# First attention of a fused attention and mixture-of-experts kernel: the sums' addition, the turn of 1/sum, and the place of the mixture's normalization

## The chip, the cores and the metric

The kernel runs on one core of one Trainium2 chip. The metric is the device time of one execution in microseconds: the median of three runs. The core has TensorE (matrix products into PSUM), VectorE, ScalarE and GpSimd (elementwise work), and queues that move data between HBM and SBUF; each engine works through its own instructions in order and waits on semaphores for the others.

## The reference

The inputs are q, k and v of 4 batches x 8 heads x 768 positions x 64, and a mixture of 4 experts over rows of 512 with a hidden width of 1024. All data are float32.

```
scores = q @ k.T / 8 - slope[head] * dist    # kept: the first 8 keys and the 96 latest
a      = exp(scores - max);  a = a / (sum(a) + 1e-9);  x = a @ v
p      = domain_probs / (domain_probs.sum(-1) + 1e-9)
out   += p[:, e] * (relu(x @ w1[e]) @ w2[e])     for each expert e
```

Here x is first brought to 3072 rows of 512, with the heads side by side. Two normalizations matter for the change: that of the attention by its sums, and that of the mixture's weights p.

## The kernel before

The attention of batch 0 has to be ready before any expert can run. `first_attention` (line 500) computes it. The attention of batches 1 to 3 (`attention`, line 420) runs later, between the products of the experts, and the change does not touch it. After these come the experts of all batches, which fill TensorE to the end of the run.

`first_attention` works on pairs of heads, each of 64, so that a pair fills 128 partitions. A pair has six tiles of 128 queries, and a step d takes two of them; four pairs make 12 steps, 0 to 11. Only the keys of a tile itself and of the block before it are looked at (for tile 0 of a pair, only its own), so a score block is 128 x 256 per head, or 128 x 128 for tile 0. The loop from line 629 runs d from 1 to 13 and holds several steps in flight. In the order of the code, pass d gives out:

- the scores of step d+1 on TensorE (`scores`, line 545);
- the softmax of step d (`softmax`, line 569): four reductions on VectorE that add the bias and find the extreme, and four exponentials on ScalarE that also sum their rows into `z`, a 128x4 tile (two tiles times two heads);
- `finish(d-3)` (line 605): the product of the unnormalized output with 1/sum on VectorE, which takes the output out of a PSUM bank;
- the turn of the probabilities of step d-1 (`turn`, line 383): up to eight transposes on TensorE, and two copies from PSUM on VectorE;
- `recip(d-1)` (line 582): 1e-9 is added to the 128x4 sums, and the reciprocal is taken, both on VectorE;
- the turn of q and k of step d+2 (`turn_qk`, line 525) on TensorE, with copies on ScalarE;
- `weigh_two(d-2)` (line 588): the products with v on TensorE, and behind them four products which turn 1/sum from partitions to columns. Each of these takes one column of `zr`, repeated 64 times, as its weights and the identity as what it moves; each runs as two passes in float32. ScalarE copies the turned result into `rT`.

The order of passes 10 to 13 differs in the place of `finish`. After some of the passes the loop at line 1279 gives out the sums and high and low parts of x that the experts' products need (`forms_of`, line 659), and generators in `chores` load and split the weights for the first experts, a part after each pass, on GpSimd and ScalarE. While `Ordered.on` is set, every engine keeps the order in which its instructions are given out. It is set from line 1273 on until the count `done` reaches `ONSTEPS` = 7 in the loop at line 1353.

`mixture` (line 277) first asks for the weights p by a DMA (at d == 9). At d == 12 it gives out four small VectorE instructions: the sum of each row's four weights, the addition of 1e-9, the reciprocal and the product. The normalized weights are first used in the second layer of the first expert unit, `second(0)` (line 926). Before that come `first(0)` and `first(1)` (line 861), the first layer of units 0 and 1. There TensorE forms seven products of blocks for a unit, VectorE adds them up, ScalarE applies the ReLU, and VectorE makes the low part of the result (`work_late`).

The pools matter too. `A.small` holds six buffers of each small tile by name, `bank.psa` and `bank.psb` one PSUM bank each, and `bank.pt` two.

Of the kernel before, what the change touches and what calls it, by code (L numbers as in the profile page):

```python
# [9 lines left out]
F32 = mybir.dt.float32  # L10
# [4 lines left out]
ALU = mybir.AluOpType  # L15
# [3 lines left out]
P = 128  # L19
# [167 lines left out]
def attn_moe_kernel(ctx: ExitStack, tc, q, k, v, n_global, n_local, domain_probs, w1, w2, out):  # L187
    nc = tc.nc
    B, H, S, D = q.shape
# [12 lines left out]
    ident = const.tile([P, P], F32, name="ident")  # L202
# [4 lines left out]
    ve, ac, po, sy, te = (Ordered(tc, e) for e in (nc.vector, nc.scalar, nc.gpsimd, nc.sync, nc.tensor))  # L207
# [3 lines left out]
    WARM = 10  # L211

    ONSTEPS = 7

    PL = P + NGLOB
    bias = {}
# [178 lines left out]
    def products_with_v(px, i, tile_):  # L395

        t, pT = tile_["t"], tile_["pT"]
        vt, vg = tile_["v"]["v"], tile_["v"]["vg"]
        w0 = 1 if t == 0 else 0
        for w in range(w0, 2):  # L400
            for j in range(2):
                te.matmul(
                    px[j * D : (j + 1) * D, i * P : (i + 1) * P],
                    vt[:, j, t] if w == 1 else vg[:, j, t - 1],
                    pT[:, w, j, :],
                    start=(w == w0),
                    stop=(w == 1),
                )
# [91 lines left out]
    def first_attention(A, bank):  # L500
# [3 lines left out]
        zs, pxs, rTs = {}, {}, {}  # L504
# [15 lines left out]
        def start_v(pr):  # L520
            vt, vg = (A.natv.tile([P, 2, NQT, D], F32, name=f"first_{m}") for m in ("v", "vg"))
            load_v(vt, vg, 0, pr)
            nats[pr]["v"], nats[pr]["vg"] = vt, vg
# [21 lines left out]
        def scores(d):  # L545

            pr, ts = tiles_of(d)
            pss = [ps_mm.tile([P, 512], F32, name="pm") for _ in range(2)]
            got, at = gots[pr], 0
            zs[d] = A.small.tile([P, 2, 2], F32, name="z")  # L550
            for t in ts:
                c0 = max(t - 1, 0) * PL + (0 if t == 0 else NGLOB)
                m = P if t == 0 else 2 * P
                for j in range(2):
                    own = slice(j * D, (j + 1) * D)
                    te.matmul(
                        pss[j][:, at : at + m],
                        got["q"][own, t * P : (t + 1) * P],
                        got["k"].rearrange("p t c -> p (t c)")[own, c0 : c0 + m],
                        start=True,  # L560
                        stop=True,
                    )
                steps.append({
                    "t": t, "i": t % 2, "pr": pr, "ps": [ps[:, at : at + m] for ps in pss], "z": zs[d],
                    "v": nats[pr],
                })
                at += m
# [12 lines left out]
                ac.activation(e, e, AF.Exp, bias=nmax[:, j : j + 1], scale=-1.0, accum_out=new["z"][:, i, j : j + 1])  # L580

        def recip(d):
            zr = A.small.tile([P, 2, 2], F32, name="zr")
            ve.tensor_scalar_add(zr, zs[d], 1e-9)
            ve.reciprocal(zr, zr)
            zs[d] = zr

        def weigh_two(d):
            pxs[d] = bank.psa.tile([P, 512], F32, name="ps")
            for tile_ in steps[2 * d : 2 * d + 2]:  # L590
                products_with_v(pxs[d], tile_["i"], tile_)
            rt = pxs[d][:, 2 * P :]
            for i in range(2):
                for j in range(2):
                    te.matmul(
                        rt[j * D : (j + 1) * D, i * P : (i + 1) * P],
                        zs[d][:, i, j : j + 1].to_broadcast([P, D]),
                        ident,
                        start=True,
                        stop=True,  # L600
                    )
            rTs[d] = A.rT.tile([P, 2 * P], F32, name="rT")
            ac.copy(rTs[d], rt)

        def finish(d):
            pr, ts = tiles_of(d)
            ve.tensor_mul(x[:, pr, ts[0] * P : (ts[1] + 1) * P], pxs[d][:, : 2 * P], rTs[d])
# [21 lines left out]
        for d in range(1, last + 3):  # L629
            if d + 1 <= last:  # L630
                scores(d + 1)
            if last - 1 <= d <= last + 1:
                finish(d - 3)
            if d <= last:
                softmax(steps[2 * d])
                softmax(steps[2 * d + 1])
            if d <= 3:
                next(spread)
            if 3 <= d < last - 1:
                finish(d - 3)  # L640
            if 1 <= d <= last + 1:
                for n in range(2):
                    turn(bank, A, steps[2 * d - 2 + n], ve.tensor_copy)
                recip(d - 1)
            if d + 2 <= last:
                turn_qk(d + 2)
            if d >= 2:
                weigh_two(d - 2)
            if d > last:
                finish(d - 2)  # L650
            if d % 3 == 1 and d // 3 + 2 < NPAIR:
                start(ORDER[d // 3 + 2], slice(0, NQT))
            if d % 3 == 2 and d // 3 + 2 < NPAIR:
                start_v(ORDER[d // 3 + 2])
            yield
# [618 lines left out]
    with ExitStack() as start_stack:  # L1274
        A = Pools(
            start_stack, "start",
            dict(setup=1, kd=2, qd=2, nat=2, natv=3, pb=6, pT=4, rT=2, small=6, sums=2), {},
        )
        for d, _ in enumerate(first_attention(A, bank)):
            if d == 0:  # L1280
                chores.append(load_w1(0, 0, 1, 1, po.tensor_copy))
            if d == 6:
                chores.append(load_w1(1, 0, 1, 0, po.tensor_copy))
            if d == 10:
                chores.append(load_w2(0, 2, (po.tensor_copy, ac.copy), 2))
            if d == 9:
                mix = mixture()
                next(mix)
            if d == 5:
                forms_of(0, ("B11", "T1"), ac.copy, po, ve, A)  # L1290
            if d == 8:
                forms_of(0, ("B21", "B22", "T3"), ac.copy, po, ve, A)
            if d == 9:
                forms_of(0, ("T2", "T4"), ac.copy, po, ve, A)
            if d == 11:
                forms_of(1, ("B11", "T1"), ac.copy, po, ve, A)
            if d == 12:
                p1, vv = up1.tile([P, HALF], F32, name="p1"), up.tile([P, HALF], F32, name="vv")
                ac.copy(p1, product(0, "A11", "B11")[:, :HALF])
                begun[1] = product(0, "A12", "B21", (0,))  # L1300
                next(mix, None)
                forms_of(1, ("B21",), ac.copy, ve, ve, A)
            if d == 13:
                begun[0] = p1, vv
                begun[2] = up1.tile([P, HALF], F32, name="p1")
                pms = product(0, "S1", "T1"), product(1, "A11", "B11")

                def take():
                    ve.tensor_add(vv, pms[0][:, :HALF], p1)
                    ac.copy(begun[2], pms[1][:, :HALF])  # L1310

                last_forms(1, take, A)
            work_chores()
    hp = early.enter_context(tc.tile_pool(name="hp", bufs=2))
    op = early.enter_context(tc.tile_pool(name="op", bufs=1))
    A = Pools(early, "att", dict(natv=1, ks=1, qs=1, nat=1, pb=2, pT=6, xt=2, small=2), {})
# [19 lines left out]
    for b in range(TURNED):  # L1336
        events = [(first, b * per)]
        for i in range(b * per + 1, (b + 1) * per):
            events += [(first, i), (second, i - 1)]
        events.append((second, (b + 1) * per - 1))  # L1340
        for n, (fn, i) in enumerate(events):
            if n == len(events) - 2:
                if b == TURNED - 1:
                    for _ in att:
                        pass
                chores.append(blocks(b + 1))
            if b == 0 and n == 0:
                chores += [load_w1(2, 1, 4, 1), load_w2(1, 6)]
            else:
                chores.append(load_w1(i + 2, 4) if fn is first else load_w2(i + 2))  # L1350
            if b == TURNED - 1 and n == len(events) - 12:
                chores.append(spread_shares())
            for _ in fn(i):
                work_chores()
                done += 1
                if done == ONSTEPS:
                    next(att)
                    check_sizes()
                    Ordered.on = False
                while emitted < count and emitted * (span - ONSTEPS) < (done - ONSTEPS) * count:  # L1360
                    next(att, None)
                    emitted += 1
# [43 lines left out]
```

## Time and profile before

| what | value |
|---|---|
| median of 3 runs | 1152.72 us (1151.89 to 1153.38) |
| profiled execution, first to last instruction (its span) | 1151.2 us |
| TensorE busy | 1133.3 us (98%) |
| VectorE busy | 890.4 us (77%) |
| GpSimd busy | 617.9 us (54%) |
| ScalarE busy | 551.7 us (48%) |
| mean granted TensorE clock | 0.999 |

The profile gives one execution on the one core. Its own time is given only as the span, from the first to the last instruction; the runs are timed around it, and their median lies 1.5 us above. In the rows, PE is TensorE, DVE VectorE, ACT ScalarE and POOL GpSimd. All instructions carry line 42, that of the helper which gives them out, so they are told apart by their tiles: `z` and `zr` are the sums and their reciprocals, `rT` the turned reciprocals, `pT` the turned probabilities, `x` the output of the attention, `T` and `xB`, `xT` the forms of x, `psumm` the mixture's sums, `zsum` the sums of the later attention, `pm`, `ps` and `pt` PSUM tiles. Where several instructions stand in one row (x2, x8) they are merged, and the time is from the first start to the last end. An instruction's recorded time can overlap the next one's start by up to a tenth of a microsecond.

### The profile page before, as it was taken

The numbers are of one execution on the slowest core, as the hardware profiler recorded it, in microseconds if no ns is written. First come the engines' busy times: TensorE is split into PE (matmuls) and PEld (weight loads), VectorE is DVE, ScalarE is ACT, GpSimd is POOL, SyncE is SP. The second block draws the span as 40 slices with busy tenths as digits, with TensorE's granted clock in tenths as the row PEclk, the third lists the DMA queues.
The fourth block names the chain that finished last, engine by engine and source line by source line (L and its number), as shares of the span: only waits on it lengthen the run. The fifth ranks groups of instructions, "written<-read, shape, count | busy, mean of one in ns | idle before, by whom it ended". The sixth has DMA issues, their size and how long they took to land.

```text
span 1151.2 us, 19555 instructions
## 1 busy us (share of the span) xinstructions
PE 1133.3 (98%) x7209; PEld 1064.8 (92%) x7209; DVE 890.4 (77%) x1618; ACT 551.7 (48%) x1337; POOL 617.9 (54%) x548
## 2 busy tenths in 40 slices
PE   8999999999999999999999999999999999999998
PEld 6778888888888889999999999999999899999996
DVE  6976677666676679788888867888889678888884
ACT  6748888788888733422222424222224253222231
POOL 5756434534343155766666357666662377766620
PEclk9999999999999999999999999999999999999999
DMA  8568887667876676666666565666666556666632
GB/s 204 138 201 312 266 258 225 222 211 220 272 252 218 209 277 231 227 222 229 243 243 241 195 211 214 227 222 224 262 239 235 213 202 234 219 233 220 219 120 95
DMA packets 184679, 256.26 MB, mean 223 GB/s; under 512 B 109216, under 2 KB 158976, under 8 KB 173568
## 3 DMA queue, kind: packets, MB, share of 16 engines
q1 hardware_dynamic: 177520, 231.34, 59.4%
q0 software_dynamic: 6048, 22.02, 5.0%
q10 hardware_dynamic: 1008, 1.57, 0.4%
q8 instruction: 59, 0.97, 0.3%
q14 instruction: 44, 0.36, 0.1%
HBM read 199.28 MB, written 55.62 MB: 221 GB/s over the span
## 4 chain that ended last, share of the span: by engine, by line
PE 83%; DVE 9%; ACT 4%; DMA 2%; issue 1%; SPq 1%; POOL 1%; ACTq 0%; DVEq 0%
PE pm L42 49%; PE pq L42 24%; PE pt L42 6%; PE ps L42 5%; DVE sumT L42 2%; DVE form L42 2%; DVE hB L42 1%; ACT pb L42 1%; DVE hT L42 1%; DMA w1s<-kept 1%; DVE pm L42 1%; DVE x L42 1%; DVE sumB L42 1%; SPq L42 1%; ACT form L42 0%
## 5 line engine op out<-in xcount | busy, mean ns | idle before, releaser
L42 PE MATMUL pm<-xT,w1s 128*128 128x384 f32 x1536 | 305.9, 336 | 0.8 <-DVE h L42 0.5
L42 PEld LDWEIGHTS pm<-xT,w1s 128*128 128x128 f32 x1536 | 268.3, 188 | 2.8 <-DVE h L42 1.6
L42 PE MATMUL pm<-xB,w1s 128*128 128x384 f32 x1152 | 224.7, 336 | 1.9 <-DVE hB L42 0.9
L42 PEld LDWEIGHTS pm<-xB,w1s 128*128 128x128 f32 x1152 | 201.0, 188 | 5.7 <-DVE hB L42 3.4
L42 POOL TENSOR_TENSOR raw<-raw 128x512 f32<-128x512 f32 x84 | 119.0, 1416 | 152.8 <-DMA raw<-in_moe_w_dram 147.8
L42 PE MATMUL pq<-form,w2s 128*128 128x384 f32 x1008 | 188.7, 334 | 0.0
L42 PEld LDWEIGHTS pq<-form,w2s 128*128 128x128 f32 x1008 | 176.0, 188 | 0.0
L42 PE MATMUL pm<-w2s,h 128*128 128x512 f32 x576 | 140.3, 395 | 1.6 <-DVE h L42 1.6
L42 PE MATMUL pq<-form,w2f 128*128 128x384 f32 x756 | 141.2, 334 | 0.0
L42 PEld LDWEIGHTS pq<-form,w2f 128*128 128x128 f32 x756 | 132.0, 188 | 0.0
L42 ACT CAST form<-hB 128x768 fp32r<-128x768 f32 x105 | 85.4, 836 | 92.4 <-DVE hB L42 92.4
L42 PEld LDWEIGHTS pm<-w2s,h 128*128 128x128 f32 x576 | 106.3, 188 | 22.9 <-POOL sums L42 1.5
L42 POOL TENSOR_TENSOR w2s<-raw,w2s 128x512 fp32r<-128x512 f32 x53 | 74.0, 1401 | 90.2 <-ACT w2s L42 78.4
L42 POOL TENSOR_TENSOR form<-hB,form 128x768 fp32r<-128x768 f32 x42 | 85.9, 2046 | 33.7 <-ACT form L42 33.7
L42 DVE TENSOR_TENSOR form<-hB,form 128x768 fp32r<-128x768 f32 x63 | 89.7, 1451 | 17.1 <-ACT form L42 16.8
L42 ACT ACTIVATE pb<-pb,nmax 128x256 f32<-128x256 f32 (+1 forms) x192 | 92.7, 488 | 11.4 <-DVE nmax L42 11.3
L42 ACT COPY p<-pm 128x384 f32<-128x384 f32 x64 | 30.7, 479 | 117.6 <-PE pm L42 117.4
L42 DVE SCALAR_TENSOR_TENSOR acc<-pm,prob,acc 128x512 f32<-128x512 f32 x90 | 67.0, 748 | 24.0 <-PE pm L42 23.1
L42 POOL TENSOR_TENSOR w2f<-raw,w2f 128x512 fp32r<-128x512 f32 x63 | 81.7, 1297 | 5.0
L42 POOL TENSOR_TENSOR w1s<-raw,w1s 128x512 fp32r<-128x512 f32 (+1 forms) x32 | 32.5, 1023 | 93.7 <-ACT w1s L42 93.3
L42 DVE TENSOR_TENSOR sumT<-pq,sumT 128x768 f32<-128x768 f32 x72 | 68.4, 950 | 17.4 <-PE pq L42 17.3
L42 DVE SCALAR_TENSOR_TENSOR hB<-pm,share 128x384 f32<-128x384 f32 x132 | 72.3, 553 | 6.7 <-PE pm L42 2.8
(157 smaller groups left out, 1795.6 us busy)
## 6 DMA issues: line engine op xcount, KB each, us to landing
w1s<-kept SPq DMA_DIRECT2D x48, 1792.0 KB, 8.6
w2s<-kept SPq DMA_DIRECT2D x126, 256.0 KB, 5.2
kept<-w1s SPq DMA_DIRECT2D x16, 1792.0 KB, 8.3
raw<-in_moe_w_dram POOLq DMA_DIRECT2D x42, 512.0 KB, 8.0
raw<-in_moe_w_dram SPq DMA_DIRECT2D x32, 512.0 KB, 4.5
kept<-w2s SPq DMA_DIRECT2D x16, 1024.0 KB, 7.1
w2s<-kept SPq DMA_DIRECT2D x6, 1024.0 KB, 4.8
v<-in_v_dram SPq DMA_DIRECT2D x12, 384.0 KB, 4.8
```

The costliest lines, as they stand in the source:

```text
L42: ins = fn(*args, **kwargs)
```

## The change

There are three edits. The addition of 1e-9 to the sums is written as an instruction with an accumulated second output, `unused`, that nothing reads. For the steps 0 to 6 (`d < WIDE`) it adds in place, and the reciprocal reads each sum 64 times over and writes a 128x256 tile `zrep`, from a pool with one buffer. `weigh_two` then turns it by two 128x128 transposes in place of the four products; for the steps 7 to 11 these remain, on a narrow `zr` as before. For the wide steps the reciprocal is given out behind `weigh_two(d-2)` of the same pass. The third edit takes the four instructions of the mixture from d == 12 and gives them out when `done` reaches 6, after the first part of `first(1)`.

```diff
+    WIDE = 7
         def recip(d):
-            zr = A.small.tile([P, 2, 2], F32, name="zr")
-            ve.tensor_scalar_add(zr, zs[d], 1e-9)
-            ve.reciprocal(zr, zr)
+            unused = A.small.tile([P, 1], F32, name="zsum")
+            if d < WIDE:
+                ve.tensor_scalar(zs[d], zs[d], 1e-9, None, op0=ALU.add, op1=ALU.add, accum_out=unused)
+                zr = A.zr.tile([P, 2, 2, D], F32, name="zrep")
+                ve.reciprocal(zr, zs[d].unsqueeze(3).to_broadcast([P, 2, 2, D]))
+            else:
+                zr = A.small.tile([P, 2, 2], F32, name="zr")
+                ve.tensor_scalar(zr, zs[d], 1e-9, None, op0=ALU.add, op1=ALU.add, accum_out=unused)
+                ve.reciprocal(zr, zr)
             zs[d] = zr
...
             for i in range(2):
+                if d < WIDE:
+                    te.transpose(rt[:, i * P : (i + 1) * P], zs[d][:, i].rearrange("p j d -> p (j d)"), ident)
+                    continue
                 for j in range(2):
...
                     turn(bank, A, steps[2 * d - 2 + n], ve.tensor_copy)
-                recip(d - 1)
+                if d > WIDE:
+                    recip(d - 1)
...
                 weigh_two(d - 2)
+            if d <= WIDE:
+                recip(d - 1)
...
-            dict(setup=1, kd=2, qd=2, nat=2, natv=3, pb=6, pT=4, rT=2, small=6, sums=2), {},
+            dict(setup=1, kd=2, qd=2, nat=2, natv=3, pb=6, pT=4, rT=2, zr=1, small=6, sums=2), {},
...
-                next(mix, None)
                 forms_of(1, ("B21",), ac.copy, ve, ve, A)
...
                 done += 1
+                if done == ONSTEPS - 1:
+                    next(mix, None)
```

## Rows read from the trace of the kernel before

**Rows 1.** Stretches: length, busy PE, PEld, DVE, ACT, POOL (instructions), clock, DMA, GB/s.

```profile
13.74:38.19 24.45, 23.31 (x256) 18.82 (x256) 21.66 (x83) 20.16 (x79) 17.66 (x21) 1.00 0.98 210
38.19:55.34 17.15, 15.12 (x168) 11.74 (x162) 16.50 (x58) 13.61 (x49) 13.17 (x16) 1.00 0.34 136
55.34:78.00 22.66, 19.55 (x134) 16.94 (x133) 17.84 (x39) 10.40 (x22) 9.57 (x11) 1.00 0.52 164
```

**Rows 2.** Chain of waits, 0 to 100 us: start, us, what.

```profile
32.99 1.90 PE ps L42 x28
```

**Rows 3.** VectorE in order of time, first regime: start, us, instruction, [idle before].

```profile
13.74 1.13 DVE L42 COPY pT<-pt 128x256 f32<-128x256 f32 x2 [1.53 <-PE pt L42]
...
19.38 0.26 DVE L42 CUSTOM_DVE_ANT_0 pb<-pm,nbias 128x128 f32<-128x128 f32 x1
...
23.13 0.39 DVE L42 CUSTOM_DVE_ANT_0 pb<-pm,nbias 128x256 f32<-128x256 f32 x1
...
24.48 0.42 DVE L42 TENSOR_TENSOR x<-ps,rT 128x256 f32<-128x256 f32 x1
...
28.82 1.29 DVE L42 COPY pT<-pt 128x512 f32<-128x512 f32 x2 [0.60 <-PE pt L42]
30.03 0.16 DVE L42 TENSOR_SCALAR zr<-z 128x4 f32<-128x4 f32 x1
...
30.32 0.53 DVE L42 TENSOR_TENSOR T<-x 128x384 f32<-128x384 f32 x1
30.76 0.28 DVE L42 CUSTOM_DVE_ANT_0 pb<-pm,nbias 128x128 f32<-128x128 f32 x1
```

**Rows 4.** VectorE in order of time, second regime.

```profile
40.13 1.29 DVE L42 COPY pT<-pt 128x512 f32<-128x512 f32 x2 [0.17 <-PE pt L42]
...
43.90 1.29 DVE L42 COPY pT<-pt 128x512 f32<-128x512 f32 x2 [0.30 <-PE pt L42]
45.10 0.97 DVE L42 TENSOR_SCALAR zr<-z 128x4 f32<-128x4 f32 x1
...
50.37 1.22 DVE L42 TENSOR_SCALAR zr<-z 128x4 f32<-128x4 f32 x1
```

**Rows 5.** GpSimd in order of time.

```profile
50.29 1.27 POOL L42 TENSOR_TENSOR w1s<-sums,w1s 128x512 fp32r<-128x512 f32 x1
```

**Rows 6.** VectorE instructions by tile: durations in ns, least, median, greatest.

```profile
L42 DVE RECIPROCAL zsum<-zsum x72: 153/156/167, 92.7 to 401.2; 128x2 f32<-128x2 f32 x72
...
L42 DVE TENSOR_SCALAR zr<-z x12: 158/478/1217, 14.8 to 56.9; 128x4 f32<-128x4 f32 x12
L42 DVE RECIPROCAL zr<-zr x12: 177/178/179, 15.0 to 57.3; 128x4 f32<-128x4 f32 x12
...
L42 DVE TENSOR_REDUCE psumm<-prob x1: 244/244/244, 58.2 to 58.2; 128x24 f32<-128x96 f32 x1
...
L42 DVE RECIPROCAL psumm<-psumm x1: 303/303/303, 59.3 to 59.3; 128x24 f32<-128x24 f32 x1
```

**Rows 7.** TensorE in order of time, step 5.

```profile
29.06 0.38 PE L42 MATMUL ps<-ident,first_q 128*128 128x128 f32 x2
...
30.29 0.61 PE L42 MATMUL ps<-ident,zr 128*64 128x128 f32 x8
```

**Rows 8.** VectorE in order of time, end of the first attention and after.

```profile
58.47 0.78 DVE L42 TENSOR_SCALAR psumm<-psumm 128x24 f32<-128x24 f32 x1
...
61.09 0.42 DVE L42 TENSOR_TENSOR x<-ps,rT 128x256 f32<-128x256 f32 x1 [0.74 <-ACT rT L42]
...
75.38 0.56 DVE L42 TENSOR_TENSOR pm<-pm,vv 128x384 f32<-128x384 f32 x1
```

**Rows 9.** ScalarE in order of time, same stretch.

```profile
76.26 0.62 ACT L42 CAST w1s<-sums 128x512 fp32r<-128x512 f32 x1 [0.28 <-POOL sums L42]
76.78 0.48 ACT L42 ACTIVATE h<-pm 128x384 fp32r<-128x384 f32 x1
```

**Rows 10.** TensorE in order of time, same stretch.

```profile
78.00 4.37 PE L42 MATMUL pm<-w2s,h 128*128 128x512 f32 x18 [1.23 <-DVE h L42]
```

## The prediction

> **What bounds the kernel now.** I read the busy shares by stretch first, then the chain of waits, then the order of time on VectorE, GpSimd and TensorE in the first attention, which is the only part that the change touches (steps 1 to 13, from about 13.7 to 61 us) besides four small instructions in the first units of the mixture of experts.
>
> The stretches show three regimes. From 13.74 to 38.19 us TensorE is busy 23.31 of 24.45 us and VectorE 21.66. From 38.19 to 55.34 VectorE is busy 16.50 of 17.15 us and TensorE 15.12. From 55.34 to 78.00 nothing is full: TensorE is idle 22.66 - 19.55 = 3.1 us [rows 1]. From 78 us on the page's slices show TensorE at 90% busy or more (98% over the whole span), so what is late at 78 us stays late to the end.
>
> In the first regime the chain runs over TensorE alone, without a gap (scores, turns, and the group to which the 1/sum products belong [rows 2]). The copies of turned probabilities on VectorE begin at 13.74 us in step 1 and at 28.82 us in step 5 [rows 3]: (28.82 - 13.74)/4 = 3.77 us a step. VectorE waits for TensorE once in each step, just ahead of these copies: 0.60 us in the row at 28.82. In the second regime the chain goes over to VectorE, and what stands out there is the addition of 1e-9 on four numbers per partition. It takes 0.97 us at 45.10 and 1.22 us at 50.37 [rows 4], against 158 ns at its shortest [rows 6]. The one at 50.37 ends at 51.59, just as the GpSimd instruction that began at 50.29 ends (51.56) [rows 5]: it waits for GpSimd.
>
> **The wide reciprocal (steps 1 to 7).** Seven of the twelve narrow reciprocals get 128x256 instead of 128x4 elements. No row has that size. Reciprocals of 2, 4 and 24 elements took 156, 178 and 303 ns [rows 6]. From 4 to 24 elements that is 125/20 = 6.25 ns an element; from 2 to 4 it is 11. So 256 elements take 178 + 252 x 6.25 = 1753 ns by the first slope and 178 + 252 x 11 = 2950 by the second. The lower end is an ordinary two-input instruction of 128x256, 0.42 us [rows 3], if the price per element were to vanish at this size. I take 1753, from the row nearest in size; it adds 1.575 us to each of seven steps.
>
> The Trainium skill, "VectorE: DVE Perf Modes", section "First, the fixed hardware budget", says that the reciprocal is an iterative divide with a repeat count of 8. At the 0.96 GHz that the page gives, an estimate of 8.33 ns an element follows, and 2.28 us for 256. The trace's 6.25 differs from it, so the sum goes by the trace; by the page it would be 7 x 0.53 = 3.7 us more.
>
> Now the sum on VectorE, from starts to starts. Four score reductions take 23.13 to 24.48 = 1.35 us (1.09 where the step holds tile 0, as two of them then last 0.26 instead of 0.39). The product with 1/sum takes a quarter of 1.35, 0.34, as it is as long. Two copies of turned tiles take 28.82 to 30.03 = 1.21 (1.05 where one is half as wide: the pair lasts 1.13 for 1.29). The addition and the narrow reciprocal together take 30.03 to 30.32 = 0.29 unstalled, so 1.865 with the wide one; the subtraction for the forms in step 5 takes 30.32 to 30.76 = 0.44 [rows 3]. From 13.74 us:
> - step 1: 1.05 + 1.865, to 16.66
> - step 2: 1.35 + 1.21 + 1.865, to 21.08
> - step 3: 1.09 + 0.34 + 1.21 + 1.865, to 25.59
> - step 4: 1.35 + 0.34 + 1.05 + 1.865, to 30.19
> - step 5: 1.35 + 0.34 + 1.21 + 1.865 + 0.44, to 35.40
> - step 6: as step 3, to 39.90
> - step 7: as step 4, to 44.51
>
> Before, VectorE came to this point at 38.19: +6.3 us. VectorE then sets the pace at 4.5 to 4.8 us a step, over TensorE's 3.77, which moreover falls.
>
> **The buffer of one.** The wide result has a single buffer, so each reciprocal waits until the two transposes of the one before it have read it; that is why it now stands behind them in the program. The transposes come after the products with v, which wait until the product with 1/sum has been taken from the same bank. On TensorE a step's group lasts 1.90 us with four turns of q and k (two pairs, about 0.43) and eight 1/sum passes (about 0.54) [rows 2, 7]; 0.93 is left for 16 products with v. So the transposes end about 0.42 + 0.05 + 0.93 + 0.38 = 1.78 us after that product's start, and VectorE wants the buffer after 0.34 + 1.21 + 0.19 = 1.74, or 1.58 where a copy is half as wide. Queued behind the wait are the next step's reductions. I take 0.2 us in steps 4 and 7, 0.4 in all; bounds: nothing, and 1 us with 0.2 in five steps.
>
> **Two transposes for eight passes.** A pair of 128x128 transposes took 0.38 us, the eight 1/sum passes 0.61 [rows 7]: 0.23 us a step less on TensorE. Where VectorE sets the pace this is worth nothing, and I count nothing; with TensorE at the end of the chain it would be 7 x 0.23 = 1.6.
>
> **The addition with an accumulated second output.** Its price is between 158 ns and the 478 ns median it had [rows 6]. The nearest row with an accumulated output is the score reduction. It took 0.42 us beside the same GpSimd work, with no long ones among the four of a step [rows 3]. So I take the short end, which is already in the 0.29 above. In the second regime that removes 0.97 - 0.16 = 0.81 and 1.22 - 0.16 = 1.06 us [rows 4]; at the other end, nothing. The Trainium skill, "SBUF — State Buffer", section "Who interferes with whom", says that this instruction can take the port pair that VectorE shares with GpSimd, but not in the form that also writes its accumulator; no row here shows that form.
>
> In steps 8 and 9 VectorE's waits for turned tiles (0.17 and 0.30 [rows 4]) go too, since TensorE has run ahead. So at 55.34 us the delay is 6.3 + 0.4 - 0.47 - 0.81 - 1.06 = +4.4 us.
>
> **The mixture.** At its old place it costs nothing: VectorE idles 0.74 us for ScalarE before the last product with 1/sum at 61.09, after these four instructions (the longest, 0.78, is again an addition) [rows 8]. At the new place it stands ahead of additions that free VectorE's results for ScalarE. The addition at 75.38 ends at 75.94; ScalarE takes its result at 76.78, after a cast that began at 76.26 [rows 8, 9], so there is 0.84 us of cover. The four take 0.24 + 0.16 + 0.30 us [rows 6] and a product about as long as the first, so 0.95 unstalled, and 1.6 with an addition of 0.78 again; some more if the product, with two inputs, waits as well. TensorE stands idle behind this at 78.00, for 1.23 us on VectorE [rows 10]. I take +0.5, between 0 and +1.2.
>
> **The sum.** +4.4 + 0.5 = +4.9 us on the profiled span of 1151.2, so 1156.1. The median of 1152.72 lies 1.5 us above that span, and I carry the 1.5 over: **1157.6 us**. Its own range is 1155.5 to 1160.
>
> **Rivals.**
> - The reciprocal is cheap at this size (faster). At 0.42 us it adds 0.24 instead of 1.575. A full step on VectorE is then 1.35 + 0.34 + 1.21 + 0.29 + 0.24 = 3.43 and TensorE's 3.54 decides: -1.6, -1.87 for the stalls, +0.5 for the mixture, or -3.0: 1149.7 us. For it: only that the small sizes may not carry over. Against it: the 20 elements between 4 and 24 cost 6.25 ns each, where a score reduction costs (0.39 - 0.26)/128 = 1.0 ns for each element more [rows 3]. It decides below about 3.5 ns an element, where 4.9/7 = 0.70 us less each makes the sum zero. Chance 0.10.
> - The reciprocal is dearer. Halfway between the two slopes, 8.6 ns, it takes 2.35 us: 7 x 0.59 = 4.1 more, 1161.7 us. For it: the slope from 2 to 4. Against: the longer arm of the rows. Chance 0.14. The skill's figure above gives nearly the same, 1161.3.
> - The delay is taken up between 55 and 78 us, where TensorE idles 3.1 us. Then +4.9 - 3.1 = +1.8: 1154.5 us. For it: some of this idle time is behind weight loads. Against it: these loads are issued only when GpSimd frees their buffer, which follows ScalarE and VectorE in program order from the last product at 61.09, so the loads move too. Chance 0.12.
>
> The forecast keeps 0.64. What a measurement of this kernel can tell from no change is 0.2%, 2.3 us: slower means above 1155.0. Faster: 0.10, the first rival. Same: 0.12, the third. Slower: 0.78, the forecast and the second. The range goes from 1154.0 to 1162.0: it leaves out the first rival and the upper half of the second.
>
> **What would show it.** A reciprocal of 128x256 near 1.75 us, seven times; copies of turned tiles 4.5 to 4.8 us apart in steps 2 to 7, with no wait for TensorE ahead of them; additions on four sums all near 0.16 to 0.25 us; the last product with 1/sum near 65.5 us instead of 61.09; the first product with w2 near 83 instead of 78.00. A reciprocal under 1 us, or a step that stays at 3.5 us, makes the prediction wrong.

## The result and the profile after

The changed kernel took 1160.63 us, the median of five runs (1159.66 to 1161.38), beside 1153.3 for the kernel before on the same chip (1151.89 to 1153.83): a ratio of 1.006, with an interval of [1.0047, 1.0072]. It is slower, by 7.3 us, where +4.9 was forecast; 1160.63 lies inside the range given, 1154.0 to 1162.0. Its profiled span is 1158.8 us against 1151.2. One run of a later experiment took 2265.91 us, about twice as long as all others; it is left out of the ranges and ratios below.

The first view is the three stretches of after. They begin and end with the same instructions as those in [rows 1]: the first copy of step 1, the end of the reciprocal of step 7, and the end of the second regime.

```profile
14.11:46.26 32.15, 25.55 (x240) 19.07 (x239) 30.05 (x89) 20.52 (x80) 20.67 (x24) 1.00 0.76 173
46.26:60.93 14.67, 12.68 (x138) 9.86 (x136) 14.35 (x62) 13.07 (x48) 10.12 (x12) 1.00 0.01 2
60.93:81.87 20.94, 19.23 (x134) 16.94 (x133) 16.98 (x41) 8.98 (x20) 5.96 (x6) 1.00 0.68 237
```

The first regime takes 32.15 us on VectorE where it took 24.45, +7.70. The second takes 14.67 for 17.15, -2.48. The third takes 20.94 for 22.66. TensorE is now the engine with time to spare in the first stretch, busy 25.55 of 32.15 us; before it was busy 23.31 of 24.45. Its granted clock is 1.00 in all three stretches, before and after, so the clock has no part in these differences.

Next is VectorE in order of time, with the steps that stand beside those of [rows 3], the last product with 1/sum beside [rows 8], and the mixture at its new place.

```profile
23.00 1.28 DVE L42 COPY pT<-pt 128x512 f32<-128x512 f32 x2
24.20 0.15 DVE L42 TENSOR_SCALAR_CACHE_REDUCE z<-z 128x4 f32<-128x4 f32 x1
...
24.64 1.75 DVE L42 RECIPROCAL zrep<-z 128x256 f32<-128x256 f32 x1 [0.29 <-PE ps L42]
...
27.63 0.42 DVE L42 TENSOR_TENSOR x<-ps,rT 128x256 f32<-128x256 f32 x1
27.97 1.01 DVE L42 COPY pT<-pt 128x256 f32<-128x256 f32 x2
28.89 0.15 DVE L42 TENSOR_SCALAR_CACHE_REDUCE z<-z 128x4 f32<-128x4 f32 x1
...
29.61 1.75 DVE L42 RECIPROCAL zrep<-z 128x256 f32<-128x256 f32 x1 [0.56 <-PE ps L42]
...
32.93 1.28 DVE L42 COPY pT<-pt 128x512 f32<-128x512 f32 x2
...
66.69 0.42 DVE L42 TENSOR_TENSOR x<-ps,rT 128x256 f32<-128x256 f32 x1 [0.97 <-ACT rT L42]
...
77.69 0.24 DVE L42 TENSOR_REDUCE psumm<-prob 128x24 f32<-128x96 f32 x1
...
78.52 0.26 DVE L42 TENSOR_TENSOR prob<-prob,psumm 128x96 f32<-128x96 f32 x1
78.70 0.55 DVE L42 TENSOR_TENSOR vv<-pm,u 128x384 f32<-128x384 f32 x1
```

The copies of turned tiles stand 4.97 and 4.96 us apart (23.00, 27.97, 32.93), where they stood 3.77 apart; over steps 2 to 7 the distance is 4.67 to 5.06. From step 2 on they no longer wait for TensorE. The idle time has gone over to the wide reciprocal, which waits for the transposes that read its one buffer: 0.29 and 0.56 us in these two steps, and 0.26, 0.29 and 0.56 in steps 2, 6 and 7. The last product with 1/sum begins at 66.69 instead of 61.09, +5.60.

By tile, the three kinds of instruction that the change brings (least, median and greatest duration in ns, first and last start), against [rows 6]:

```profile
L42 DVE TENSOR_SCALAR_CACHE_REDUCE z<-z x7: 140/147/148, 15.2 to 43.9; 128x4 f32<-128x4 f32 x7
...
L42 DVE RECIPROCAL zrep<-z x7: 1752/1753/1754, 15.3 to 44.6; 128x256 f32<-128x256 f32 x7
L42 DVE TENSOR_SCALAR_CACHE_REDUCE zr<-z x5: 141/146/147, 49.1 to 62.5; 128x4 f32<-128x4 f32 x5
```

TensorE in order of time, first around a wait for the buffer, and then at the points where the delay is carried on:

```profile
28.11 0.44 PE L42 MATMUL ps<-pT,first_vg 128*64 128x128 f32 x4 [1.20 <-DVE x L42]
...
29.13 0.44 PE L42 MATMUL ps<-ident,zrep 128*128 128x128 f32 x2
...
81.87 8.43 PE L42 MATMUL pm<-w2s,h 128*128 128x512 f32 x36 [0.51 <-DVE h L42]
...
102.21 0.33 PE L42 MATMUL pt<-ident,pb 128*128 128x128 f32 x1 [0.54 <-ACT pb L42]
...
103.35 5.61 PE L42 MATMUL pm<-w2s,h 128*128 128x512 f32 x24
```

The two transposes of 128x256 numbers begin at 29.13, behind the products with v that began at 28.11. They end at 29.57, and the reciprocal starts at 29.61. TensorE had waited 1.20 us for VectorE ahead of these products, as the row at 28.11 shows. The products with w2 begin at 81.87 instead of 78.00 [rows 10], only 3.87 us late: 1.73 of the 5.60 has been regained. What differs there is ScalarE's order, first in the kernel before and then in after:

```profile
72.73 0.62 ACT L42 CAST w2s<-raw 128x512 fp32r<-128x512 f32 x1 [2.07 <-DMA raw<-in_moe_w_dram]
73.26 0.48 ACT L42 ACTIVATE h<-pm 128x384 fp32r<-128x384 f32 x1
```

```profile
75.77 0.96 ACT L42 ACTIVATE h<-pm 128x384 fp32r<-128x384 f32 x2 [1.10 <-DVE pm L42]
79.91 0.49 ACT L42 ACTIVATE h<-pm 128x384 fp32r<-128x384 f32 x1 [3.19 <-DVE pm L42]
80.30 0.61 ACT L42 CAST w2s<-raw 128x512 fp32r<-128x512 f32 x1
```

Before, the cast of w2 stood ahead of a ReLU and waited 2.07 us for its DMA; the ReLU behind it came late, and TensorE idled 1.23 us before the products with w2 [rows 10]. After, the two ReLUs run together and the cast comes behind another, without a wait. (The section on the kernel before says that every engine keeps the order given out while `Ordered.on` is set. As the code reads, the cast is given out behind that ReLU in both kernels, so on ScalarE the kernel before did not keep it here.)

By 103 us the gain is gone. The next products with w2 begin at 103.35 in after; in the kernel before:

```profile
97.77 5.65 PE L42 MATMUL pm<-w2s,h 128*128 128x512 f32 x24
```

That is 5.58 us late. In after TensorE waits 0.33, 0.24 and 0.54 us between 95 and 102.21, where the kernel before has no wait. The reciprocals of the later attentions, first at 92.7 and last at 401.2 before [rows 6], show what is left:

```profile
L42 DVE RECIPROCAL zsum<-zsum x72: 151/157/167, 99.2 to 407.1; 128x2 f32<-128x2 f32 x72
```

They are 6.5 and 5.9 us late. From the last of them to the end of the span 1.7 us more come in (751.7 us for 750.0). Over the eleven profiles this tail is 749.4 to 750.9 us in the five kernels without the two transposes and 750.6 to 751.7 in the six with them, one execution of each, so I count the 1.7 as unexplained.

### The profile page after: what moved, and what is told of

Its sections match the earlier page's. It is cut to its first block, busy times and chain, and to the rows that moved or that the text cites. A ratio compares the mean times of both kernels' runs of the same rounds, so it can differ in the third digit from the quotient of the medians.

```text
span 1158.8 us, 19487 instructions
## 1 busy us (share of the span) xinstructions
PE 1134.6 (98%) x7167; PEld 1063.2 (92%) x7167; DVE 894.8 (77%) x1630; ACT 550.5 (48%) x1337; POOL 617.8 (53%) x548
## 4 chain that ended last, share of the span: by engine, by line
PE 81%; DVE 10%; ACT 4%; DMA 3%; issue 1%; POOL 1%; SPq 1%; ACTq 0%; DVEq 0%
PE pm L42 48%; PE pq L42 24%; PE pt L42 5%; PE ps L42 4%; DVE sumT L42 2%; DVE hB L42 1%; DMA w1s<-kept 1%; ACT pb L42 1%; DVE form L42 1%; DVE zrep L42 1%; DVE pb L42 1%; DVE hT L42 1%; DVE x L42 1%; DVE sumB L42 1%; SPq L42 1%
## 5 line engine op out<-in xcount | busy, mean ns | idle before, releaser
L42 ACT ACTIVATE pb<-pb,nmax 128x256 f32<-128x256 f32 (+1 forms) x192 | 92.7, 487 | 19.2 <-DVE nmax L42 19.2
L42 DVE TENSOR_TENSOR form<-hB,form 128x768 fp32r<-128x768 f32 x63 | 85.5, 1384 | 17.9 <-ACT form L42 17.6
```

The lines of the kernel that those rows point to most:

```text
L42: ins = fn(*args, **kwargs)
```

## The experiments

Each was run 5 to 11 times beside the kernel before; the ratio is to that kernel, with its 95% interval. The times of single instructions come from one profiled execution each. In three of these (the addition alone, VectorE's time alone, and the copy with the old place of the mixture) the granted clock is 0.73 to 0.76 from 8 to 12 us and 0.84 or 0.50 from 12 to 16, ahead of every instruction that the edit touches, and 1.00 in the other eight. Their first copies of turned tiles begin at 15.01, 16.20 and 16.19 us instead of 13.74, so their later times hold a delay that the edit did not make. The names of the parts: the wide part (wide reciprocal and two transposes), the addition (with the unread sum) and the mixture (its four instructions moved).

**Without the wide part** (edit against after):

```diff
-    WIDE = 7
+    WIDE = 0
```

> The changed kernel with no wide step: all twelve steps keep the 128x4 reciprocal and the four products; the addition with the unread sum and the moved mixture stay. Theory (the wide reciprocal on VectorE makes the loss): the last product with 1/sum falls from 66.69 us back to about 59.5, under the 61.09 of before, since two waits of 0.81 and 1.06 us for GpSimd are gone; time 1151 to 1152. Rival (the loss lies in the moved mixture and in the order of the work after 66 us): the time stays near 1159 to 1161.

Measured: 1156.18 us (1154.88 to 1158.49), ratio 1.0025 [1.0013, 1.0036]. The last product with 1/sum came at 59.56, 1.5 us earlier than before, as the theory had it; but the time did not follow, and neither the theory's time nor the rival's was met. TensorE, in order of time, shows where the gain went:

```profile
77.83 8.43 PE L42 MATMUL pm<-w2s,h 128*128 128x512 f32 x36 [2.02 <-DVE h L42]
```

It idles 2.02 us for VectorE ahead of the products with w2, where the kernel before idles 1.23, and begins them only 0.17 us earlier than before. This profile is of one of the two shortest runs (1154.9 us, mean clock 1.000); the other five took 1155.7 to 1158.5 at 0.994 to 0.998, where most runs of the kernel before have 0.999, so part of the median is the clock. By subtraction the wide part would make 0.35 of the 0.60% (1.006 less 1.0025); alone, below, it makes 0.71, so the parts act on each other. The other two parts together still lose, and the mixture became the suspect.

**Two buffers for the wide result** (edit against after; the copy rT gives up its second buffer to make room):

```diff
-            ... pT=4, rT=2, zr=1, small=6, sums=2), {},
+            ... pT=4, rT=1, zr=2, small=6, sums=2), {},
```

> The changed kernel with two buffers for the wide reciprocal (and one for the turned 1/sum, to make room). Theory: the five waits for TensorE ahead of the wide reciprocals, 1.96 us together, go, and the last product comes 1.9 us earlier, near 64.8; time 1158.7. Rival (VectorE then only waits elsewhere, ahead of the copies of turned tiles, because TensorE is behind): nothing gained, 1160.6.

Measured: 1158.52 us (1158.04 to 1158.58), 1.0044 [1.003, 1.0058]. VectorE in order of time, step 4 and the last product:

```profile
27.95 0.15 DVE L42 TENSOR_SCALAR_CACHE_REDUCE z<-z 128x4 f32<-128x4 f32 x1
...
28.14 1.75 DVE L42 RECIPROCAL zrep<-z 128x256 f32<-128x256 f32 x1
...
64.46 0.42 DVE L42 TENSOR_TENSOR x<-ps,rT 128x256 f32<-128x256 f32 x1 [0.97 <-ACT rT L42]
```

The reciprocal follows its addition at once, in every step, VectorE waits for no other engine from the first copy to 50 us, and the last product comes 2.23 us earlier than in after, 1.8 of them since the first copy (13.65 us here, 14.11 in after). The median falls by 2.1, to within 0.2 us of the theory. The two ratios' intervals overlap, but the place and the size agree: the single buffer costs about 2 us.

**A narrow reciprocal, widened by a copy** (edit against after, with two buffers):

```diff
-                ve.reciprocal(zr, zs[d].unsqueeze(3).to_broadcast([P, 2, 2, D]))
+                inv = A.small.tile([P, 2, 2], F32, name="zinv")
+                ve.reciprocal(inv, zs[d])
+                ve.tensor_copy(zr, inv.unsqueeze(3).to_broadcast([P, 2, 2, D]))
```

> The changed kernel, but the wide tile is made by a 128x4 reciprocal and a copy of it 64 times over (128x256) on VectorE, with two buffers; the two transposes stay. Theory (only the price per element of the reciprocal is at fault): a step falls to about 3.5 us on both engines, the last product comes before 58 us, time 1149 to 1150. Rival (the copy, which reads and writes SBUF alone, waits for GpSimd as the old addition did): up to 0.5 us a step more, time 1152 to 1153.

Measured: 1152.84 us (1151.45 to 1154.24), 0.9994 [0.9985, 1.0003]: no difference from before. The theory's time was missed and the rival's met; the last product comes at 59.73, not before 58. VectorE in order of time, a step of the first regime, and the copies by tile:

```profile
29.23 1.29 DVE L42 COPY pT<-pt 128x512 f32<-128x512 f32 x2
...
30.62 0.18 DVE L42 RECIPROCAL zinv<-z 128x4 f32<-128x4 f32 x1
30.84 0.29 DVE L42 COPY zrep<-zinv 128x256 f32<-128x256 f32 x1
...
32.96 1.28 DVE L42 COPY pT<-pt 128x512 f32<-128x512 f32 x2
```

```profile
L42 DVE COPY zrep<-zinv x7: 293/303/519, 15.1 to 38.1; 128x256 f32<-128x256 f32 x7
```

The 128x256 instruction takes 0.29 us in place of 1.75, and the copies of turned tiles are 3.73 us apart (29.23, 32.96). With two buffers in both, this kernel against the one above gives the price of the wide reciprocal over the narrow one with its copy: 1.0044 less 0.9994, 0.5% or 5.8 us. The copy takes up to 519 ns.

Here TensorE runs the middle steps without a wait, so its scores show what the transposes save. The same scores of the kernel before, three steps apart, and then of this kernel:

```profile
27.27 0.93 PE L42 MATMUL pm<-early_k,early_q 64*128 64x128 f32 x8
...
38.58 0.93 PE L42 MATMUL pm<-early_k,early_q 64*128 64x128 f32 x8
```

```profile
27.68 0.93 PE L42 MATMUL pm<-early_k,early_q 64*128 64x128 f32 x8
...
38.79 0.93 PE L42 MATMUL pm<-early_k,early_q 64*128 64x128 f32 x8
```

Three steps take 11.11 us instead of 11.31. Two transposes for eight passes save 0.07 us a step, 0.5 us in seven steps, and a step takes 3.70 us and not 3.5.

**The wide part alone** (edit against after; likewise for the narrow `zr`, and the mixture is at its old place):

```diff
-                ve.tensor_scalar(zs[d], zs[d], 1e-9, None, op0=ALU.add, op1=ALU.add, accum_out=unused)
+                ve.tensor_scalar_add(zs[d], zs[d], 1e-9)
```

> The kernel before with the wide reciprocal and the transposes alone: the addition without the unread sum, the mixture in its old place. Theory (wide steps lose about 7.5 us, the other two edits give back about 2 in the first attention): 1162 to 1163, and some additions last 0.5 to 1.2 us again. Rival (the moved mixture costs what is lost beyond the 5.6 us at the last product, about 2 us): 1159 to 1161.

Measured: 1161.0 us (1160.95 to 1163.24), 1.0071 [1.0058, 1.0085]: at the upper end of the rival's range, 1 us under the theory's. By tile:

```profile
L42 DVE TENSOR_SCALAR z<-z x7: 157/523/994, 15.1 to 45.0; 128x4 f32<-128x4 f32 x7
L42 DVE TENSOR_SCALAR zr<-z x5: 158/434/1212, 50.2 to 65.0; 128x4 f32<-128x4 f32 x5
```

The additions are back at up to 994 and 1212 ns, and the last product with 1/sum comes at 69.27, 8.2 us later than before and 2.6 later than in after, yet the time is no more than in after: the products with w2 begin at 83.77, 5.77 us later than before. So 2.4 us are regained here, and TensorE has no wait ahead of them.

**The addition alone** (edit against before):

```diff
-            ve.tensor_scalar_add(zr, zs[d], 1e-9)
+            unused = A.small.tile([P, 1], F32, name="zsum")
+            ve.tensor_scalar(zr, zs[d], 1e-9, None, op0=ALU.add, op1=ALU.add, accum_out=unused)
```

> The kernel before with the addition that writes an unread sum, and nothing else. Theory: additions last 0.15 us each and no longer wait for GpSimd, the last product with 1/sum comes 1.5 us earlier (59.6 us, as with no wide step), and since the mixture stays where it was this reaches the end: 1151.5 to 1152. Rival (ScalarE's cast of the second expert weights, which waits for its data in this order, takes the gain back before 80 us): 1153.

Measured: 1151.82 us (1151.12 to 1153.24), 0.9986 [0.9977, 0.9995]. It beats both kernels, the one before by 1.5 us, as the theory had it. By tile:

```profile
L42 DVE TENSOR_SCALAR_CACHE_REDUCE zr<-z x12: 140/147/148, 16.1 to 56.1; 128x4 f32<-128x4 f32 x12
```

All twelve additions take 140 to 148 ns, where they took up to 1217 [rows 6]. The last product comes at 60.26, 0.83 us earlier than before. In this execution the copies of step 2 begin 0.67 us later than before (18.18 for 17.51, behind the low clock), so from there on 1.50 us are gained, as the theory had it; the products with w2 begin at 77.50, 0.50 earlier, behind a wait of 1.61 us for 1.23, so part of the gain is lost there, as the rival had it. What the additions waited for shows in the kernel before: seven of the twelve, and the mixture's, last 0.44 us or more, and each of these eight ends 0.02 to 0.04 us after a GpSimd instruction that had begun before it.

**The mixture alone** (edit against before):

```diff
@@ d == 12
-                next(mix, None)
@@ after done += 1
+                if done == ONSTEPS - 1:
+                    next(mix, None)
```

> The kernel before with the four mixture instructions moved, and nothing else. Theory: the last product stays at 61.1 us, and the first product with w2 comes 1.2 to 1.4 us after 78.0, because VectorE's 1.0 to 1.6 us stand ahead of the additions that ScalarE waits for: 1154.5. Rival (VectorE waits there anyway): 1153.3, no change.

Measured: 1157.22 us (1155.36 to 1158.6), 1.003 [1.002, 1.0041]. Both expectations were too low: moving four instructions costs 3.9 us. VectorE in order of time, and TensorE at the products with w2:

```profile
73.74 0.56 DVE L42 SCALAR_TENSOR_TENSOR h<-pm,h 128x384 fp32r<-128x384 f32 x1 [1.68 <-ACT h L42]
74.22 0.24 DVE L42 TENSOR_REDUCE psumm<-prob 128x24 f32<-128x96 f32 x1
...
75.08 0.64 DVE L42 TENSOR_TENSOR prob<-prob,psumm 128x96 f32<-128x96 f32 x1
75.64 0.55 DVE L42 TENSOR_TENSOR vv<-pm,u 128x384 f32<-128x384 f32 x1
```

```profile
79.57 10.03 PE L42 MATMUL pm<-w2s,h 128*128 128x512 f32 x36 [2.02 <-DVE h L42]
```

VectorE has just waited 1.68 us for ScalarE when the four come in, ahead of the addition chain that TensorE needs; the product among them takes 0.64, and ends 0.12 us after a GpSimd instruction that ran beside it (75.72 for 75.60). In after, where GpSimd stands idle from 74.03 to 80.99, the product takes 0.26. TensorE then stands 2.02 us. In this profile the 36 products that follow take 10.03 us, where they take 8.43 in the kernel without the wide part. The granted clock in the stretches (the last number but two) says why:

```profile
78.00:81.00 3.00, 1.43 (x6) 1.24 (x7) 2.00 (x5) 2.09 (x5) 3.00 (x5) 0.99 0.92 218
81.00:84.00 3.00, 3.00 (x8) 2.31 (x7) 1.32 (x3) 0.00 (x0) 3.00 (x5) 0.50 0.75 178
```

After an idle stretch (1.43 us busy of 3.00) the granted clock is 0.50 for the next 3 us, the 1.2 GHz level. The kernel without the wide part had the same idle time of 2.02 us and kept its clock in the profiled run, so this does not come each time. It seems to come often: the mean clock is 0.996 to 0.998 in all eight runs of this kernel and 0.994 to 0.998 in five of seven of that one, and 0.999 or 1.000 in all five of after. Where in those runs the clock fell is not shown.

**VectorE's time alone** (edit against before: seven wide reciprocals whose results are not read; eight 1/sum passes, old addition, old mixture):

```diff
             ve.tensor_scalar_add(zr, zs[d], 1e-9)
+            rTs[d] = A.rT.tile([P, 2 * P], F32, name="rT")
+            if d < 7:
+                ve.reciprocal(rTs[d].rearrange(...), zr.unsqueeze(3).to_broadcast([P, 2, 2, D]))
             ve.reciprocal(zr, zr)
...
-            rTs[d] = A.rT.tile([P, 2 * P], F32, name="rT")
```

> The kernel before with seven reciprocals of 128x256 more on VectorE in steps 1 to 7, whose results are overwritten unread; TensorE's products, the additions and the mixture stay as they were. Theory (time on VectorE alone makes the loss): the last product comes 6 to 7 us later, 67 to 68 us, and the time is 1159 to 1160.5. Rival (what is lost is bound to the transposes, their buffer or the order after): the last product moves by less than 3 us and the time stays under 1157.

Measured: 1162.77 us (1161.71 to 1164.9), 1.0081 [1.0068, 1.0095]: more than the theory, and the rival is refuted. VectorE at the last product, and two stretches of four microseconds below full speed:

```profile
73.08 0.42 DVE L42 TENSOR_TENSOR x<-ps,rT 128x256 f32<-128x256 f32 x1 [0.78 <-ACT rT L42]
```

```profile
12.00:16.00 4.00, 3.26 (x15) 2.04 (x14) 1.18 (x8) 2.76 (x11) 0.22 (x1) 0.50 1.07 266
...
46.00:50.00 4.00, 2.49 (x24) 2.43 (x24) 3.97 (x13) 2.85 (x11) 2.55 (x4) 0.69 0.67 287
```

The last product comes 11.99 us later than before, not 6 to 7. Of these, 2.46 stand ahead of the first copy (16.20 for 13.74), behind the first low stretch and before the first wide reciprocal at 18.36; 9.53 are left. The profile is of the longest run (1164.9 us, mean clock 0.994); three of the five ran at 0.997 to 0.998 and took 1161.7 to 1162.8. So part of the size is the clock. Another part may be that the seven narrow reciprocals stay beside the wide ones here, 0.18 us each. For both reasons this kernel does not tell, set beside the wide part alone, what the transposes save. But it has the four products and the cast of w2 ahead of the ReLU, and the products with w2 begin at 89.92, 11.92 later than before: of a delay twice that of after next to nothing is regained.

**The narrow reciprocal with a copy, and the old place of the mixture** (edit against the copy's kernel):

```diff
@@ d == 12
+                next(mix, None)
@@ after done += 1
-                if done == ONSTEPS - 1:
-                    next(mix, None)
```

> The unread sum, the narrow reciprocal with a copy 64 times over, and two transposes in seven steps, but the mixture in its old place. Theory (the moved mixture costs about 1 us wherever VectorE is ahead of ScalarE): 1 us under the same kernel with the mixture moved, 1151.5 to 1152. Rival (the order of ScalarE's work that comes with the moved mixture is worth as much): 1152.8 again.

Measured: 1152.42 us (the median of all eleven; 1150.32 to 1154.24 without the one long run), 0.9987 [0.9978, 0.9996]: also a little better than both kernels, equal to the addition alone (0.9986), and between the two expectations. So even without the dear reciprocal the two transposes with their copies add nothing to what the addition brings. The copies take more here than in the kernel above:

```profile
L42 DVE COPY zrep<-zinv x7: 293/561/1196, 18.1 to 40.8; 128x256 f32<-128x256 f32 x7
```

The three longest end 0.15 or 0.16 us after a GpSimd instruction that had begun before them, as the rival on the copy had it.

**After, with the mixture at its old place** (the same edit, against after):

> The changed kernel with the mixture in its old place (wide reciprocals, transposes and the unread sum stay). The mixture alone cost 3.9 us on the kernel before. Theory (it costs so much only in that order of ScalarE's work, where a cast that waits for its data holds a ReLU and TensorE then idles; in the changed kernel the ReLU goes first): 1159.5 to 1160.5, at most 1 us under the changed kernel. Rival (the prices add up, and the moved mixture makes half of the loss): 1157.

Measured: 1158.39 us (1157.17 to 1159.44), 1.0043 [1.0029, 1.0057]; after has 1.006 [1.0047, 1.0072]. TensorE reaches the products with w2 without a wait:

```profile
80.63 8.36 PE L42 MATMUL pm<-w2s,h 128*128 128x512 f32 x36
```

That is 1.24 us earlier than in after, of which 0.58 was there already at the last product with 1/sum (66.11 for 66.69). The last twelve products of the next unit with w2 begin 1.91 us earlier (108.74 for 110.65). The medians are 2.2 us apart; the intervals overlap. The time lies between the two expectations, and the interval decides for neither.

## Why the prediction was right, and where its sizes were off

- **The wide reciprocal.** Seven of 1752 to 1754 ns, against 1753 worked out from the slope between 4 and 24 elements. Both rivals on its price fall. The Trainium skill, "VectorE: DVE Perf Modes", section "First, the fixed hardware budget", by the estimate of 8.33 ns an element would have made it 2.28 us and the sum 3.7 us more; the measurement decides for 6.25 ns.
- **VectorE sets the pace of steps 2 to 7.** Right, though the steps take 4.67 to 5.06 us and not 4.5 to 4.8. The time by the sum of instructions was 24.45 + 6.3 = 30.77 us for the first regime; without the buffer waits it is 32.15 - 1.96 = 30.19. Of the 0.58 between them, 0.25 is that a pair of copies with a half-wide one takes 0.92 us from start to start (27.97 to 28.89), not 1.05, in steps 4 and 7, though not in step 1. Another 0.2 is that the waits are counted from the end of the addition, and so hold the 0.04 us that pass there in a step without a wait too.
- **The buffer of one: the mis-sized term.** The prediction took 0.4 us, between 0 and 1.0. Measured: 0.26 + 0.29 + 0.56 + 0.29 + 0.56 = 1.96 us in five of six steps. The product with 1/sum begins at 27.63 and the transposes end 1.94 us later, not 1.78: the products with v begin 0.48 after it and not 0.47, but 1.02 pass until the transposes begin and not 0.93, and these last 0.44 and not 0.38. VectorE wants the buffer earlier, as the copies and the addition are shorter: 28.89 + 0.15 = 29.04, 1.41 after the product and not 1.58. Two terms nearly equal were subtracted (1.78 and 1.74), and the error of each went into the difference whole. The wait is thus above the upper bound given, 1 us. Two buffers took it away, and 2.1 us of the median with it.
- **Transposes for passes.** Nothing was counted. That is right where VectorE sets the pace alone: with two buffers it waits for no one in the wide steps, and TensorE waits for it 0.67 to 1.21 us in four of them. With one buffer the transposes stand inside the wait, as the point above has it. The 0.23 us a step that TensorE was to save is wrong, and with it the 3.54 us a step of the first rival. It set the lengths of the rows (0.61 and 0.38) against each other. From start to start the passes take 0.54 us (18.98 to 19.52 in the kernel before) and the transposes 0.37 (19.69 to 20.06 in the copy's kernel), and the transposes begin 0.10 us later behind the last products with v. That leaves 0.07 us a step, as measured.
- **The addition.** Predicted 0.16 us unstalled, measured 0.14 to 0.15. The second regime fell by 2.48 us, where 0.47 + 0.81 + 1.06 = 2.34 were taken off. The Trainium skill, "SBUF — State Buffer", section "Who interferes with whom", says that the form that also writes its accumulator does not take the port pair that VectorE shares with GpSimd; the trace agrees, with 148 ns at the longest for up to 1217.
- **At the last product with 1/sum.** +5.60 us, where 4.4 was predicted: +1.56 for the buffer, -0.58 for the rest of the first regime, -0.14 for the stalls, +0.37 for a later first copy (14.11 for 13.74, in this profile), which makes 5.6.
- **From there to the end.** The prediction carried the delay one to one. The rival that it is taken up between 55 and 78 us happened in part, by 1.73 us at the products with w2 (at 81.87, where near 83 was forecast), not behind weight loads but with ScalarE's other order; at the next products with w2 the delay was 5.58 again. Carried whole is right in the end, by luck: what was regained was lost again on a path that the prediction did not have.
- **The mixture.** The sign was right. In after its four instructions take 1.01 us (77.69 to 78.70) with no stall, near the 0.95 worked out, and cost 0.7 us at the products with w2 (1.24 - 0.58) and 1.3 at the next unit's (1.91 - 0.58); the medians say 2.2. The price seems to go with ScalarE's order; that pairing is read from the runs, and no run changed the order alone. With the four products, where the cast of w2 comes first, the move costs 0.30% (alone) and 0.39% (without the wide part against the addition alone, 1.0025 less 0.9986). With the two transposes, where ReLUs come first, it costs 0.17% (after, 1.006 less 1.0043) and 0.07% (with the copy, 0.9994 less 0.9987), neither apart from nothing by the intervals. Two more things go with the first order, so how much of the difference is the order's stays open: the product of the four runs beside GpSimd and takes 0.64 and 0.84 us instead of 0.26, and the mean clock is 0.998 or lower in 13 of the 15 runs of the two kernels with the move, against 2 of the 21 runs of the three with the move and the transposes. The cover of 0.84 us was read for the first order; that the order would change was not foreseen.

The parts don't add up: alone they give +0.71, -0.14 and +0.30%, or +0.87% together, and after has 0.60%. The four intervals together leave about 0.2% to chance. That the mixture costs less in the kernels with the transposes would explain part of the rest.

What stays open: the 1.7 us of the tail, and why moving from four products to two transposes changes the order of the cast and the ReLU. It does so in each of the six kernels with transposes and in none of the five without, whatever the mixture does; what fixes this order was not examined.

## What to carry to other kernels

Work out the price per element of a reciprocal from two sizes in your own trace. Take it narrow and widen the result by a copy, 0.18 + 0.29 us here for 1.75, but count on the copy to last longer beside GpSimd (up to 1.20 us here). Of all that was tried nothing beat the addition alone, which needs no wide tile. Take the price of an instruction from start to start, not from the length of its row. Time taken off an engine is worth nothing where the replacement makes its neighbour the one that sets the pace. Where two arrival times differ by less than their error, take the wait's bound from that error, and buy the second buffer if there is room.

## What the runs showed of the hardware

- A 128x256 reciprocal took 1753 ns and a 128x256 copy with the same repeated reading of four numbers 293 ns unstalled: the width costs 6.25 ns an element in the one and little in the other. Beside GpSimd the copy took up to 1196 ns.
- The unread accumulated sum adds an 80 ns instruction of its own behind the addition (the profile shows it at 24.27, within the addition's 24.20 to 24.35) and removes waits of up to 1.06 us. Alone it is worth 0.14% [0.05%, 0.23%].
- Two 128x128 transposes behind products of 64 columns began 0.32 us after the start of the last four products (19.37 to 19.69 in the copy's kernel), where products of 64 columns again began after 0.22 (18.76 to 18.98 before).
- After 2.02 us of idle time TensorE's granted clock was 0.50 (the 1.2 GHz level) for about 3 us in one kernel's profile, at a cost of some 1.6 us (10.03 less 8.43), and 1.00 in another's after the same idle time.
- In three of eleven profiles the granted clock was 0.73 to 0.76 from 8 to 12 us, after a stretch from 4 to 8 us in which TensorE was as busy (3.26 us of 4) as in kernels that kept 1.00 (3.27 before). The code that runs there is the same in all eleven; what decides it is not shown.
